# One change to a transformer block on Trainium2: chunk 0's attention scores summed on TensorE, and weighted values added up on VectorE instead of by DMA

## The chip, the cores and the metric

The kernel runs on one core of a Trainium2 chip. The metric is the device time of one execution in microseconds (us). Before the change three runs took 797.45, 798.05 and 800.79 us, with a median of 798.05.

Five engines of a core work side by side, each through its own queue, in the order of the program: TensorE (PE in the profile; PEld are its weight loads), VectorE (DVE), ScalarE (ACT), GpSimd (POOL) and SyncE (SP). SP, POOL and ACT also start DMA transfers. Semaphores make an instruction wait for those that it depends on; whatever stands behind it on its engine waits too.

## The reference

x has 2048 rows of 1024 values. The block is attention and then a feed-forward part, each with a layer norm ahead of it and a residual sum behind it. Attention is local and dilated: each row looks at itself and at the rows 2, 4, ... 14 before it (W = 8), in 32 heads of 32 values.

```python
H = 32; Dh = D // H
W, dil = 8, 2
q, k, v = ...            # layernorm(x) @ wqkv, split into heads
idx = pos[:, None] - off[None, :]
mask = idx >= 0
logits = jnp.einsum("bhsd,bhswd->bhsw", q, kg) * scale
logits = jnp.where(mask[None, None, :, :], logits, -1e9)
attn = _softmax(logits, axis=-1)
o = jnp.einsum("bhsw,bhswd->bhsd", attn, vg)
# h  = x + o @ wo
# h2 = h + ((ln(h) @ w_gate) * (ln(h) @ w_up)) @ w_down
```

`kg` and `vg` are k and v, gathered at the eight rows of each position.

## The kernel before

The 2048 rows are cut into four chunks of 512 (TC). Matrix products run on TensorE in groups of eight matmuls of 128x512, one group per 128 output columns; a group takes 1.73 us (`GROUP_US`). Results come out in PSUM, which has eight banks of 128x512 fp32 here (the pool with tag "mm"); a bank is free for a new group when the engine that reads it is done.

**Order of the groups.** `qkv(c, blocks)` is the projection of chunk c: blocks 0 and 1 are q, 2 and 3 are k, 4 and 5 are v, four groups each. The program runs, on TensorE: chunk 0's block 0, then its blocks 1 to 3; chunk 1's blocks 0 to 3; chunk 0's v; chunk 1's v; chunks 2 and 3 (L729 to L752). Then come the output projection of chunk 0 (`wo_ln2(0)`), chunk 3's v, gate and up products of chunk 0 (`ffn1(0)`), `wo_ln2(1)`, the down products of chunk 0 in two halves (`ffn2`), `ffn1(1)`, and a long second part for the remaining rows in which attention has no share, except that chunk 3's values are wanted by `wo_adds(2)` and `wo_adds(3)`.

**Layouts.** A projection group leaves 128 channels (4 heads of 32) on the partitions and 512 rows along the free dimension. `evac_qkv` (L305) has ScalarE copy it from PSUM to a tile `sg`, and SP store it to DRAM (`qd`, `kd`, `vd`). POOL loads it again (`load_qk`, `load_v`, L411 to L421) with another layout: a partition is a quarter of the chunk and a head, and the free dimensions are the 32 channels and 128 rows. The tiles `qD`, `kD`, `vD`, `oD`, `prod`, `lg` have one buffer each (pool `att`).

**Attention** (L427) is a generator. In that layout a product with a shifted window of k is one VectorE instruction over 4096 elements (L434), and the sum over a head's 32 channels is a tree of additions (L436 to L444), for two of the eight window positions at a time. Softmax follows (L446 to L462). Then v is multiplied with the weights: per pair of positions two products (L479) and one addition of the two (L483), and a DMA on POOL's queue that writes the first pair to `od` and adds each later pair to what lies there (L484). The pair's result is in `pv` (which has the buffer of `prod`) for even pairs and in `oD` for odd ones. At the end POOL loads `od` back as `oT` for the output projection (L489) and then the next chunk's v.

**What sets the order.** The program places VectorE's background work between TensorE's groups by a scheduler, `Background` (L37). After each group of 1.73 us, `bg.step` adds that much credit (4.0 us at most) and takes pieces from the first generator that is ready until the credit is spent; a `yield 2.3` charges 2.3 us, a `yield "later", 1.0` gives the turn away for 1 us. `bg.spend` charges VectorE work that the main program places itself. `bg.rate` is 1 until `wo_ln2(0)` and 0.98 from there. All this happens when the program is written out; on the chip VectorE runs its queue in that order, at whatever speed it reaches. Instructions of the main program stand in the same queue: the additions of the output projection (L514), the products of gate and up (L597), and the four stores of each half of `ffn2` (L617), all of which free or follow PSUM banks.

At the start the generators `rows_gen` (layer norms of chunks 1 and 2) are in the list; `start_attention(0)` (L737) stands after chunk 0's k and gives the generator a start 16 us later; `stats_gen(norm1[3])`, the statistics of chunk 3, is added at L736.

Of the kernel before, what the change touches and what calls it, by code (L numbers as in the profile page):

```python
# [8 lines left out]
BF = mybir.dt.bfloat16  # L9
F32 = mybir.dt.float32  # L10
I32 = mybir.dt.int32
F16 = mybir.dt.float16
ALU = mybir.AluOpType
# [7 lines left out]
DH = 32  # L21
F = 3584
W = 8
DIL = 2
HB = 16
TC = 512
NCH = S // TC
SUB = TC // 4
KO = D // 128
NF = F // 128  # L30
NP = NF // 2
EPS = 1e-5
NEG = -1.0e9
GROUP_US = 1.73


# [42 lines left out]
def kernel(  # L79
# [11 lines left out]
    nc = tc.nc  # L91
# [11 lines left out]
    t1k = ctx.enter_context(tc.tile_pool(name="t1k", bufs=30))  # L103
    small = ctx.enter_context(tc.tile_pool(name="small", bufs=4))
    att = ctx.enter_context(tc.tile_pool(name="att", bufs=1))
    psum = ctx.enter_context(tc.tile_pool(name="psum", bufs=8, space=PSUM))
# [13 lines left out]
    od = [dram.tile([4, H, DH, SUB], BF, name=f"od{c}") for c in range(NCH)]  # L120

    bg = Background()
# [4 lines left out]
        return wt, src  # L127

    stream = []
    for b in range(6):  # L130
        stream.append((("qkv", b), wqkv_v[:, :, bass.ts(b, 512)], KO))
    def stream_wo(c):
        for hf in range(2):
# [39 lines left out]
    def retire(n=1):  # L173
        state["live"] -= n
        pump()
# [116 lines left out]
    halo = const.tile([128, 16, HB], BF)  # L292
    nc.gpsimd.memset(halo[:], 0.0)
    mask = const.tile([32, W, 16], F32)
    nc.gpsimd.memset(mask[:], 0.0)
    for w in range(1, W):
        nc.gpsimd.memset(mask[:, w, 0:DIL * w], NEG)

    wps = psum.tile([128, 512], F32, tag="mm", name="warm_ps")
    for i in range(13):  # L300
# [2 lines left out]
    qkv_in = {}  # L303

    def evac_qkv(c, m, ps):  # L305
        sg = t1k.tile([128, HB + TC], BF, tag="t1k", name=f"sg{c}_{m}")
        nc.scalar.copy(sg[:, HB:HB + TC], ps[:])  # L307
        hg = m % 8
        if m >= 8:
            nc.scalar.copy(sg[:, 0:HB], halo[:, m - 8, :])  # L310
            if c + 1 < NCH:
                nc.scalar.copy(halo[:, m - 8, :], ps[:, TC - HB:TC])
        if m < 8:
            nc.sync.dma_start(qd[c][:, 4 * hg:4 * hg + 4, :, :].rearrange("c g d s -> (g d) c s"),
                              sg[:, HB:HB + TC].rearrange("p (c s) -> p c s", c=4))
            return
        dst = (kd, vd)[m // 8 - 1][c]
        base = sg[:, 0:1]
        win = bass.AP(base.tensor, base.offset, [list(base.ap[0]), [SUB, 4], [1, SUB + HB]])
        nc.sync.dma_start(dst[:, 4 * hg:4 * hg + 4, :, :].rearrange("c g d s -> (g d) c s"), win)  # L320
# [76 lines left out]
    def qkv(c, blocks, last=False):  # L397
        for b in blocks:
            for j in range(4):
                ps = psum.tile([128, TC], F32, tag="mm", name=f"ps{c}_{b}_{j}")  # L400
                mm_group(ps, wts["qkv", b], j, lnTs[c])
                evac_qkv(c, b * 4 + j, ps)
                bg.step(GROUP_US)
            if last:
                retire()
# [5 lines left out]
    def load_qk(c):  # L411
        qD = att.tile([128, DH, SUB], BF, tag="qD", name=f"qD{c}")
        kD = att.tile([128, DH, SUB + HB], BF, tag="kD", name=f"kD{c}")
        nc.gpsimd.dma_start(qD[:], qd[c].rearrange("c g d s -> (c g) d s"))
        nc.gpsimd.dma_start(kD[:], kd[c].rearrange("c g d s -> (c g) d s"))
        qkv_in["q", c], qkv_in["k", c] = qD, kD
# [7 lines left out]
        if c in stored and ("q", c) not in qkv_in:  # L424
            load_qk(c)

    def attention(c):  # L427
        qD, kD = qkv_in["q", c], qkv_in["k", c]
        lg = att.tile([128, W, SUB], F32, tag="lg", name=f"lg{c}")
        for wp in range(W // 2):  # L430
            prod = att.tile([128, 2, DH, SUB], BF, tag="prod", name=f"prod{c}_{wp}")
            for j in range(2):
                o = HB - DIL * (2 * wp + j)
                nc.vector.tensor_tensor(prod[:, j], qD[:], kD[:, :, o:o + SUB], ALU.mult)  # L434
                yield 2.3
            nc.vector.tensor_tensor(prod[:, :, 0:16], prod[:, :, 0:16], prod[:, :, 16:32], ALU.add)  # L436
            yield 2.3
            nc.vector.tensor_tensor(prod[:, :, 0:8], prod[:, :, 0:8], prod[:, :, 8:16], ALU.add)
            yield 1.2
            t3 = att.tile([128, 2, 4, SUB], F32, tag="t3", name=f"t3{c}_{wp}")  # L440
            nc.vector.tensor_tensor(t3[:], prod[:, :, 0:4], prod[:, :, 4:8], ALU.add)
            yield 1.2
            nc.vector.tensor_tensor(t3[:, :, 0:2], t3[:, :, 0:2], t3[:, :, 2:4], ALU.add)
            nc.vector.tensor_tensor(lg[:, 2 * wp:2 * wp + 2, :], t3[:, :, 0], t3[:, :, 1], ALU.add)  # L444
            yield 1.0
        if c == 0:  # L446
            nc.vector.tensor_tensor(lg[0:32, :, 0:16], lg[0:32, :, 0:16], mask[:], ALU.add)
        tr = att.tile([128, 4, SUB], F32, tag="t3", name=f"tr{c}")
        nc.vector.tensor_tensor(tr[:], lg[:, 0:4], lg[:, 4:8], ALU.max)
        nc.vector.tensor_tensor(tr[:, 0:2], tr[:, 0:2], tr[:, 2:4], ALU.max)  # L450
        mx = att.tile([128, SUB], F32, tag="mx", name=f"mx{c}")
        nc.vector.tensor_tensor(mx[:], tr[:, 0], tr[:, 1], ALU.max)
        nc.vector.tensor_tensor(lg[:], lg[:], mx[:, None, :].to_broadcast((128, W, SUB)), ALU.subtract)
        nc.scalar.activation(lg[:], lg[:], ACTF.Exp, scale=float(DH) ** -0.5)
        yield 3.5
        tr2 = att.tile([128, 4, SUB], F32, tag="t3", name=f"trs{c}")
        nc.vector.tensor_tensor(tr2[:], lg[:, 0:4], lg[:, 4:8], ALU.add)
        nc.vector.tensor_tensor(tr2[:, 0:2], tr2[:, 0:2], tr2[:, 2:4], ALU.add)
        sm = att.tile([128, SUB], F32, tag="mx", name=f"sm{c}")
        nc.vector.tensor_tensor(sm[:], tr2[:, 0], tr2[:, 1], ALU.add)  # L460
        rs = att.tile([128, SUB], F32, tag="rs", name=f"rs{c}")
        nc.vector.reciprocal(rs[:], sm[:])  # L462
        yield 2.5
        prefetch_qk(c + 1)
        while ("v", c) not in qkv_in:
            yield "later", 1.0
        vD = qkv_in["v", c]
        at = att.tile([128, W, SUB], BF, tag="at", name=f"at{c}")
        nc.vector.tensor_tensor(at[:], lg[:], rs[:, None, :].to_broadcast((128, W, SUB)), ALU.mult)
        yield 1.2  # L470
        pv = att.tile([128, 2, DH, SUB], BF, tag="prod", name=f"pv{c}")
        oD = att.tile([128, DH, SUB], BF, tag="oD", name=f"oD{c}")
        odv = od[c].rearrange("c g d s -> (c g) d s")
        for wp in range(W // 2):
            a, b = (oD[:] if wp % 2 else pv[:, 0]), pv[:, 1]
            for j, p in enumerate((a, b)):
                w = 2 * wp + j
                o = HB - DIL * w
                nc.vector.tensor_tensor(p, vD[:, :, o:o + SUB],  # L479
                                        at[:, w, None, :].to_broadcast((128, DH, SUB)), ALU.mult)  # L480
                yield 2.3
            prefetch_qk(c + 1)
            nc.vector.tensor_tensor(a, a, b, ALU.add)  # L483
            nc.gpsimd.dma_start(odv, a, max_dma_last_dim=4096,  # L484
                                accum_op=ALU.bypass if wp == 0 else ALU.add)
            yield 2.3
        oT = att.tile([128, KO, 4, SUB], BF, tag="oT", name=f"oT{c}")
        for cp in range(4):
            nc.gpsimd.dma_start(oT[:, :, cp, :], od[c][cp].rearrange("(hg hl) d s -> (hl d) hg s", hl=4))  # L489
        oTs[c] = oT  # L490
        while c + 1 < NCH and ("q", c + 1) not in qkv_in:
            yield "later", 1.0
            prefetch_qk(c + 1)
        if c + 1 < NCH:
            load_v(c + 1)
# [3 lines left out]
    def wo_ln2(c):  # L499
# [8 lines left out]
        for t in range(4):  # L508
            for hf in range(2):
# [12 lines left out]
                bg.spend(0.7)  # L522
                bg.step(GROUP_US)
        norm(3)
# [57 lines left out]
    def ffn1(c, lnT, at={}):  # L582
        hT = []
        for b in range(7):
            if b == 5 and c + 1 < NCH:
                hss[c + 1] = load_x(c + 1, "h", nc.sync)
            for j in range(4):
# [3 lines left out]
                nc.scalar.copy(gs[:], pg[:])  # L591
                bg.step(GROUP_US)
                pu = psum.tile([128, TC], F32, tag="mm", name=f"pu{c}_{b}_{j}")
# [5 lines left out]
                bg.spend(0.45)  # L599
                bg.step(GROUP_US)  # L600
                hT.append(gs)
# [120 lines left out]
    atts = {}  # L722

    def start_attention(c):
        stored.add(c)
        atts[c] = attention(c)
        bg.add(atts[c], bg.now + (16.0 if c == 0 else 0.0))

    qkv(0, range(1, 4))  # L729
    load_qk(0)  # L730
    bg.finish(rows2)
    for t in range(4):
        norm1[2].transpose(t)
    xtiles[3] = load_x(3, "x", nc.sync)
    pump(6)
    bg.add(stats_gen(norm1[3]), bg.now + 6.0)  # L736
    start_attention(0)  # L737
    qkv(1, range(4))
    qkv(0, range(4, 6))
    load_v(0)  # L740
# [85 lines left out]
    def wo_adds(c, at):  # L826
        hs = hss[c]
        for t in range(4):
            for hf in range(2):
# [5 lines left out]
                bg.spend(0.7)  # L835
                bg.step(GROUP_US)
                if 2 * t + hf in at:
# [237 lines left out]
    for q in range(4):  # L1075
        dprod(ps_x[q], q, S1, fcells(t1h), True)
        p = lnp.tile([128, TC], F32, tag="ln", name=f"dp5_{q}")
# [60 lines left out]
```

## Time and profile before

| | |
|---|---|
| median of three runs | 798.05 us |
| the profiled execution | 798.05 us |
| its span, first to last instruction | 796.2 us |
| TensorE's granted clock, mean | 0.989 of full |
| DMA moved | 146.96 MB, 185 GB/s |

Each engine's busy time over 40 slices of 19.9 us shows where it is full; a digit is tenths. A row of VectorE, for comparison with TensorE's:

```profile
DVE  5629998899988989779978429996544444478953
```

The costs of the operations that the change touches are rows of the list of groups: line, engine, operation, output and inputs, count, then busy us in total and mean ns of one, and the idle time ahead of them:

```profile
L434 DVE TENSOR_TENSOR prod<-qD,kD 128x4096 bf16<-128x4096 bf16 x32 | 72.4, 2284 | 11.5 <-DMA od<-pv 8.5
...
L479 DVE TENSOR_TENSOR pv<-vD,at 128x4096 bf16<-128x4096 bf16 x24 | 54.5, 2286 | 1.8 <-DMA od<-pv 1.7
...
L436 DVE TENSOR_TENSOR prod<-prod 128x4096 bf16<-128x4096 bf16 x16 | 36.6, 2290 | 0.4
```

A wait is read as "engine, line of the waiting instruction, what it waited for". In the order of time of one engine each row is start, duration, engine, line, operation; what stands in brackets is the idle time just before it and what ended that.

### The profile page before, as it was taken

To read this page: it belongs to the slowest core of one execution; us is meant where nothing else is said; L and a number is where in the kernel's file an instruction comes from. 1 tells how busy PE (TensorE), PEld (TensorE's weight loads), DVE (VectorE), ACT (ScalarE), POOL (GpSimd) and SP (SyncE) were. 2 spreads that over 40 slices of the span, in tenths; PEclk is the share of its full clock that TensorE was granted. 3 is DMA by queue.
4 is the path that set the end of the run, shared out by engine and by line. 5 is a ranking of instruction groups with operands and counts; after the bars stand their busy time and mean duration, and the time that the engine had idled before them with its cause. 6 is when DMAs were issued, how large, how long until landed. Compare 5 with 4: busy or idle time off the path is not lost.

```text
span 796.2 us, 10374 instructions
## 1 busy us (share of the span) xinstructions
PE 771.4 (97%) x3632; PEld 354.6 (45%) x3691; DVE 586.0 (74%) x770; ACT 471.0 (59%) x1021; POOL 157.5 (20%) x164
## 2 busy tenths in 40 slices
PE   9999999997999999994999999999999999999998
PEld 6444444443444444441444444444444444444444
DVE  5629998899988989779978429996544444478953
ACT  5626444312666642972787789855777777779140
POOL 0000001200012000002001001005877776800000
PEclk9999999999999999997999999999999999999999
DMA  8998799998999965999467976274233233550001
GB/s 284 261 246 197 173 270 193 279 293 222 304 257 255 307 245 152 266 226 321 137 186 232 259 260 187 58 167 133 74 86 105 63 98 106 190 181 28 0 27 54
DMA packets 187492, 146.96 MB, mean 185 GB/s; under 512 B 81456, under 2 KB 176688, under 8 KB 185904
## 3 DMA queue, kind: packets, MB, share of 16 engines
q1 hardware_dynamic: 176912, 110.12, 49.3%
q0 software_dynamic: 7360, 34.61, 16.6%
q10 hardware_dynamic: 3168, 1.57, 0.8%
q8 instruction: 29, 0.48, 0.3%
q14 instruction: 23, 0.19, 0.1%
HBM read 104.86 MB, written 34.60 MB: 175 GB/s over the span
## 4 chain that ended last, share of the span: by engine, by line
PE 41%; DVE 11%; DMA 3%; ACT 1%; issue 1%; SPq 0%; DVEq 0%; ACTq 0%
PE dx L787 6%; PE pz L680 6%; PE py L680 6%; PE pg L394 6%; PE px L680 6%; PE pu L394 6%; PE pv L680 3%; PE dy L787 3%; DMA lx<-in_B_w_down_dram 2%; DMA od<-pv 1%; DVE prod L434 1%; DVE h L834 1%; DVE prodx L780 1%; DVE w_dn L780 1%; DVE st L181 1%
## 5 line engine op out<-in xcount | busy, mean ns | idle before, releaser
L394 PE MATMUL ps<-lnT,w_qkv 128*128 128x512 bf16 x720 | 159.0, 379 | 3.6 <-DVE h L514 2.0
L394 PE MATMUL pg<-lnT,w_wg 128*128 128x512 bf16 x439 | 108.3, 388 | 13.9 <-DVE h L617 10.6
L394 PEld LDWEIGHTS <-w_qkv 128*128 128x128 bf16 x736 | 71.9, 98 | 89.4 <-issue 3.7
L394 PE MATMUL pu<-lnT,w_wu 128*128 128x512 bf16 x439 | 106.3, 382 | 0.5
L307 ACT CAST sg<-ps 128x512 bf16<-128x512 f32 x96 | 54.7, 589 | 50.5 <-PE ps L394 47.2
L434 DVE TENSOR_TENSOR prod<-qD,kD 128x4096 bf16<-128x4096 bf16 x32 | 72.4, 2284 | 11.5 <-DMA od<-pv 8.5
L394 PEld LDWEIGHTS <-w_wg 128*128 128x128 bf16 x448 | 44.3, 99 | 68.5 <-issue 17.5
L394 PEld LDWEIGHTS <-w_wu 128*128 128x128 bf16 x448 | 44.3, 99 | 54.2 <-issue 2.4
L680 PEld LDWEIGHTS <-sw 128*128 128x128 f16 x448 | 43.8, 98 | 53.5 <-issue 0.9
L596 ACT CAST us<-pu 128x512 bf16<-128x512 f32 x56 | 33.1, 591 | 42.6 <-PE pu L394 41.5
L479 DVE TENSOR_TENSOR pv<-vD,at 128x4096 bf16<-128x4096 bf16 x24 | 54.5, 2286 | 1.8 <-DMA od<-pv 1.7
L680 PE MATMUL px<-lnT,ws 128*128 128x512 bf16 x212 | 53.1, 379 | 0.6
L680 PEld LDWEIGHTS <-ws 128*128 128x128 f16 x336 | 32.9, 98 | 39.6
L626 PE MATMUL acc<-w_wd,gs 128*128 128x512 bf16 x220 | 48.5, 379 | 0.4 <-DVE h L514 0.2
L661 POOL TENSOR_TENSOR sw<-ws 128x512 f16<-128x512 f16 x26 | 30.0, 1153 | 84.8 <-PE py L680 77.5
L591 ACT CAST gs<-pg 128x512 bf16<-128x512 f32 x56 | 32.7, 584 | 21.5 <-PE pg L394 19.6
L185 ACT ACTIVATE rs<-mv,eps 128x1 f32<-128x1 f32 (+1 forms) x25 | 7.4, 297 | 60.3 <-DVE mv L182 55.3
L597 DVE TENSOR_TENSOR gs<-gs,us 128x512 bf16<-128x512 bf16 x56 | 23.4, 419 | 26.1 <-ACT us L596 26.0
L484 POOL DMA_DIRECT2D od<-pv x8 | 7.7, 958 | 164.6 <-DVE pv L483 128.6
L436 DVE TENSOR_TENSOR prod<-prod 128x4096 bf16<-128x4096 bf16 x16 | 36.6, 2290 | 0.4
L540 ACT ACTIVATE junkd<-w_wd 128x512 bf16<-128x512 bf16 x56 | 34.3, 613 | 0.0
L626 PEld LDWEIGHTS <-gs 128*128 128x128 bf16 x224 | 21.9, 98 | 26.8 <-issue 0.5
(313 smaller groups left out, 1383.9 us busy)
## 6 DMA issues: line engine op xcount, KB each, us to landing
w_wg<-in_B_w_gate_dram SPq DMA_DIRECT2D x14, 1024.0 KB, 9.1
w_wu<-in_B_w_up_dram SPq DMA_DIRECT2D x14, 1024.0 KB, 6.0
od<-pv POOLq DMA_DIRECT2D x8, 1024.0 KB, 8.8
od<-oD POOLq DMA_DIRECT2D x8, 1024.0 KB, 10.1
w_wd<-in_B_w_down_dram SPq DMA_DIRECT2D x8, 896.0 KB, 6.5
w_pair<-in_B_w_gate_dram SPq DMA_DIRECT2D x14, 512.0 KB, 4.0
w_pair<-in_B_w_up_dram SPq DMA_DIRECT2D x14, 512.0 KB, 5.3
w_wo<-in_A_wo_dram SPq DMA_DIRECT2D x6, 1024.0 KB, 10.2
```

Of the source, the lines that this page charges most:

```text
L307: nc.scalar.copy(sg[:, HB:HB + TC], ps[:])
L394: nc.tensor.matmul(ps[:], lhsT=wt[:, ko, bass.ts(j, 128)], rhs=rhs[:, ko, :], start=(ko == 0), stop=(ko == KO - 1))
L434: nc.vector.tensor_tensor(prod[:, j], qD[:], kD[:, :, o:o + SUB], ALU.mult)
L436: nc.vector.tensor_tensor(prod[:, :, 0:16], prod[:, :, 0:16], prod[:, :, 16:32], ALU.add)
L479: nc.vector.tensor_tensor(p, vD[:, :, o:o + SUB], at[:, w, None, :].to_broadcast((128, DH, SUB)), ALU.mult)
L540: nc.scalar.activation(junk, src, ACTF.Abs, accum_out=self.l1[:, k:k + 1])
L591: nc.scalar.copy(gs[:], pg[:])
L596: nc.scalar.copy(us[:], pu[:])
L626: nc.tensor.matmul(acc[t][:], lhsT=hT[f][:, bass.ts(t, 128)], rhs=wts["wd", c, hf, b][:, j, :], start=(f == 0), stop=(f == NF - 1))
L661: eng.tensor_tensor(sw[:, i, 0], a21, a22, ALU.add)
L680: nc.tensor.matmul(ps[:], lhsT=lhs[:, ko, :], rhs=rhs[:, ko, :], start=(fresh and ko == 0), stop=(ko == 3), skip_group_check=not fresh)
L787: nc.tensor.matmul(ps[:, bass.ds(lo, n)], lhsT=lhs[k][:, bass.ts(q, 128)], rhs=rhs[k][:, bass.ds(lo, n)], start=(fresh and k == 0), stop=( ...
```

## The change

Chunk 0's q and k are no longer stored and loaded again. ScalarE copies them from PSUM into `qT` and `kT` (in the buffers of `qD` and `kD`), channels on the partitions. `natural_logits` multiplies them on VectorE in this layout: two groups of 128 channels and four window positions in one instruction, eight instructions in all, into four buffers (two halves of `prod`, and those of `oD` and `vD`). TensorE sums over a head's channels: `heads` has a 1 where a channel belongs to a head, 32 columns wide, and each matmul (128x32 weights, 512 columns) writes 32 partitions of PSUM, one quarter of the chunk. A reduction is eight such matmuls, two channel groups by four quarters; there are eight. Reduction i is placed behind product i + 2. Two PSUM banks hold the sums until ScalarE copies them to `lg`. The window positions come in the order `NAT`, which mask and weighted values follow. Chunk 0's k block 2 is projected ahead of q block 1, its weights are loaded earlier, and attention of chunk 0 starts right behind it.

In all four chunks the weighted values are no longer added up by DMA: later pairs are added to `oD` by one more VectorE instruction each, three per chunk, and `od` is written once.

```diff
-    for b in range(6):
+    for b in (0, 2, 1, 3, 4, 5):
         stream.append((("qkv", b), wqkv_v[:, :, bass.ts(b, 512)], KO))
...
+    heads = t1k.tile([128, KO, 32], BF, tag="t1k", name="heads")
+    nc.gpsimd.memset(heads[:], 0.0)
+    for i in range(4):
+        base = heads[32 * i:32 * i + 32, 0, i:i + 1]
+        nc.gpsimd.memset(bass.AP(base.tensor, base.offset, [list(base.ap[0]), [36, KO]]), 1.0)
+    qT = att.tile([128, KO, TC], BF, tag="qD", name="qT")
+    kT = att.tile([128, KO, HB + TC], BF, tag="kD", name="kT")
+    nc.gpsimd.memset(kT[:, :, 0:HB], 0.0)
+    natural = set()
...
     def evac_qkv(c, m, ps):
+        if c == 0 and m < 16:
+            natural.add(m)
+            if m < 8:
+                nc.scalar.copy(qT[:, m, :], ps[:])
+            else:
+                nc.scalar.copy(kT[:, m - 8, HB:HB + TC], ps[:])
+                nc.scalar.copy(halo[:, m - 8, :], ps[:, TC - HB:TC])
+            return
...
+    def natural_logits(lg):
+        room = att.tile([128, 2, 2, 4, TC], BF, tag="prod", name="nprod")
+        bufs = [room[:, 0], room[:, 1], att.tile([128, 2, 4, TC], BF, tag="oD", name="nprod_o")[:],
+                att.tile([128, 2, 4, TC], BF, tag="vD", name="nprod_v")[:]]
+        acc = [psum.tile([128, 4, SUB], F32, tag="mm", name=f"lgp{i}") for i in range(2)]
+
+        def reduce(i):
+            for g in range(2):
+                hg = i // 2 * 2 + g
+                for cp in range(4):
+                    rows = slice(32 * cp, 32 * cp + 32)
+                    nc.tensor.matmul(acc[i % 2][rows], lhsT=heads[:, hg, :], rhs=bufs[i % 4][:, g, :, bass.ts(cp, SUB)],
+                                     start=(hg == 0), stop=(hg == KO - 1))
+
+        for i in range(8):
+            hg = i // 2 * 2
+            while not {hg, hg + 1, hg + 8, hg + 9} <= natural:
+                yield "later", 1.0
+            base = kT[:, hg, HB - DIL * (i % 2 * 4 + 3):HB]
+            win = bass.AP(base.tensor, base.offset, [list(base.ap[0]), [HB + TC, 2], [DIL, 4], [1, TC]])
+            nc.vector.tensor_tensor(bufs[i % 4], qT[:, hg:hg + 2, None, :].to_broadcast((128, 2, 4, TC)), win, ALU.mult)
+            yield 2.3
+            if i > 1:
+                reduce(i - 2)
+        yield "later", 2.0
+        reduce(6)
+        nc.scalar.copy(lg[:, 0:4], acc[0][:])
+        yield "later", 2.0
+        reduce(7)
+        nc.scalar.copy(lg[:, 4:8], acc[1][:])
...
         for wp in range(W // 2):
-            a, b = (oD[:] if wp % 2 else pv[:, 0]), pv[:, 1]
-            for j, p in enumerate((a, b)):
+            pv = att.tile([128, 2, DH, SUB], BF, tag="prod", name=f"pv{c}_{wp}")
+            for j in range(2):
                 w = 2 * wp + j
-                o = HB - DIL * w
-                nc.vector.tensor_tensor(p, vD[:, :, o:o + SUB],
+                o = HB - DIL * order[w]
+                nc.vector.tensor_tensor(pv[:, j], vD[:, :, o:o + SUB],
                                         at[:, w, None, :].to_broadcast((128, DH, SUB)), ALU.mult)
                 yield 2.3
             prefetch_qk(c + 1)
-            nc.vector.tensor_tensor(a, a, b, ALU.add)
-            nc.gpsimd.dma_start(odv, a, max_dma_last_dim=4096,
-                                accum_op=ALU.bypass if wp == 0 else ALU.add)
-            yield 2.3
+            if wp == 0:
+                nc.vector.tensor_tensor(oD[:], pv[:, 0], pv[:, 1], ALU.add)
+                yield 2.3
+            else:
+                nc.vector.tensor_tensor(pv[:, 0], pv[:, 0], pv[:, 1], ALU.add)
+                yield 2.3
+                nc.vector.tensor_tensor(oD[:], oD[:], pv[:, 0], ALU.add)
+                yield 2.3
+        nc.gpsimd.dma_start(od[c].rearrange("c g d s -> (c g) d s"), oD[:])
...
-        bg.add(atts[c], bg.now + (16.0 if c == 0 else 0.0))
-
-    qkv(0, range(1, 4))
-    load_qk(0)
+        bg.add(atts[c], bg.now)
+
+    qkv(0, (2,))
+    start_attention(0)
+    qkv(0, (1, 3))
...
-    start_attention(0)
```

More of the change, by code (lines that the diff above doesn't have):

```diff
@@ L33 @@
 NEG = -1.0e9
+NAT = (3, 2, 1, 0, 7, 6, 5, 4)
 GROUP_US = 1.73
@@ L295 @@
     nc.gpsimd.memset(mask[:], 0.0)
-    for w in range(1, W):
-        nc.gpsimd.memset(mask[:, w, 0:DIL * w], NEG)
+    for i, w in enumerate(NAT):
+        if w:
+            nc.gpsimd.memset(mask[:, i, 0:DIL * w], NEG)
+    heads = t1k.tile([128, KO, 32], BF, tag="t1k", name="heads")
[7 more added lines that the diff above has]
+    natural = set()
     wps = psum.tile([128, 512], F32, tag="mm", name="warm_ps")
@@ L425, in prefetch_qk, with logits @@
             load_qk(c)
-    def attention(c):
+    def natural_logits(lg):
[26 more added lines that the diff above has]
+        nc.scalar.copy(lg[:, 4:8], acc[1][:])
+    def logits(c, lg):
         qD, kD = qkv_in["q", c], qkv_in["k", c]
-        lg = att.tile([128, W, SUB], F32, tag="lg", name=f"lg{c}")
         for wp in range(W // 2):
@@ L445, in attention @@
             yield 1.0
+    def attention(c):
+        lg = att.tile([128, W, SUB], F32, tag="lg", name=f"lg{c}")
+        order = range(W) if c else NAT
+        yield from logits(c, lg) if c else natural_logits(lg)
         if c == 0:
@@ L470, in attention @@
         yield 1.2
-        pv = att.tile([128, 2, DH, SUB], BF, tag="prod", name=f"pv{c}")
         oD = att.tile([128, DH, SUB], BF, tag="oD", name=f"oD{c}")
-        odv = od[c].rearrange("c g d s -> (c g) d s")
         for wp in range(W // 2):
-            a, b = (oD[:] if wp % 2 else pv[:, 0]), pv[:, 1]
-            for j, p in enumerate((a, b)):
+            pv = att.tile([128, 2, DH, SUB], BF, tag="prod", name=f"pv{c}_{wp}")
+            for j in range(2):
                 w = 2 * wp + j
-                o = HB - DIL * w
-                nc.vector.tensor_tensor(p, vD[:, :, o:o + SUB],
+                o = HB - DIL * order[w]
+                nc.vector.tensor_tensor(pv[:, j], vD[:, :, o:o + SUB],
                                         at[:, w, None, :].to_broadcast((128, DH, SUB)), ALU.mult)
```

## The prediction

> **What bounds the kernel now.** I read the page's span and slices first, then who TensorE waited for, then the stretches around its gaps, then VectorE in order of time through the largest gap.
>
> ```profile
> span 796.2 us, 10374 instructions
> ...
> PE 771.4 (97%) x3632; PEld 354.6 (45%) x3691; DVE 586.0 (74%) x770; ACT 471.0 (59%) x1021; POOL 157.5 (20%) x164
> ...
> PE   9999999997999999994999999999999999999998
> ```
>
> TensorE is the bound: busy in every slice but two, the tenth and the nineteenth. Time can only come out of those two holes, and whatever TensorE gets in addition is paid in full. Who it waits for (engine, line, waited-for: us, times, longest):
>
> ```profile
> PE pg L394 <- DVE h L617: 10.6, 1, 10.6
> PE pg L394 <- DMA lnT<-ln: 2.9, 1, 2.9
> PE ps L394 <- DVE h L514: 2.0, 2, 1.1
> ...
> PE ps L394 <- ACT sg L307: 0.7, 1, 0.7
> ```
>
> The stretches (busy us and count of PE, PEld, DVE, ACT, POOL; then the granted clock and DMA):
>
> ```profile
> 178.80:196.90 18.10, 14.14 (x62) 6.11 (x64) 17.25 (x26) 4.93 (x18) 1.07 (x2) 0.99 0.86 212
> 196.90:200.20 3.30, 3.27 (x9) 1.19 (x10) 3.16 (x5) 0.00 (x0) 0.00 (x0) 0.52 1.02 344
> 364.80:375.40 10.60, 0.03 (x1) 0.03 (x1) 10.43 (x9) 1.62 (x3) 0.00 (x0) 0.62 1.06 314
> 375.40:381.60 6.20, 6.20 (x17) 2.20 (x17) 6.20 (x7) 0.58 (x1) 0.00 (x0) 0.55 0.80 261
> ```
>
> After each hole TensorE runs at about half clock: the next groups of eight matmuls take 3.4 us instead of 1.73. VectorE meanwhile is full. Its order of time, and its waits:
>
> ```profile
> 337.28 2.29 DVE L479 TENSOR_TENSOR oD<-vD,at 128x4096 bf16<-128x4096 bf16 x1 [4.94 <-DMA od<-oD]
> ...
> 349.16 2.29 DVE L434 TENSOR_TENSOR prod<-qD,kD 128x4096 bf16<-128x4096 bf16 x1 [5.06 <-DMA od<-pv]
> ...
> 351.37 2.48 DVE L617 TENSOR_TENSOR h<-acc,h 128x512 bf16<-128x512 f32 x4
> ...
> 374.63 2.48 DVE L617 TENSOR_TENSOR h<-acc,h 128x512 bf16<-128x512 f32 x4
> ```
>
> ```profile
> DVE oD L479 <- DMA od<-oD: 11.9, 4, 4.9
> ...
> DVE prod L434 <- DMA od<-pv: 8.5, 2, 5.1
> ...
> DVE pv L479 <- DMA od<-pv: 1.7, 1, 1.7
> ```
>
> The cause is a lag. The background scheduler places attention instructions in VectorE's queue at the pace of TensorE's groups, by nominal costs; it knows nothing of VectorE's waits for the accumulating writes to `od`. Each such wait makes VectorE later than its place in the program, and the lag stays. The second half's stores (L617) belong at TensorE's 357.7 us and run at 374.6: 17 us late. They free the PSUM banks of `acc`, so TensorE stands from 364.8.
>
> **What is there to win.** (a) Chunk 0's output projection: 16 groups of 1.73 us from 163.8 would end at 191.5; the first `pg` starts at 196.93, 5.4 late, and its eight matmuls lose 3.43 - 1.73 = 1.7 to the clock: 7.1. (b) The hole at 364.8: 10.6, then two groups in 3.37 and 2.84 instead of 1.73 each, 2.75: 13.4. (c) 0.7 at 60.1 us, where ScalarE's PSUM copies stood behind statistics of chunk 3 that waited for x. Together 21.2 us.
>
> **What the Trainium skill says.** "TensorE: Matmul & The Clock Gate", Part 1, has the half clock after an idle window of about 3.4 us; the trace agrees (0.55 after 10.6 us). Part 3 of that page says that matmuls with outputs in different 32-column groups run concurrently, 2.38 times as fast for three tiles of N=512; no instruction of this trace shows it. "TensorEngine Tiling (Array Packing)", Key Properties, says that a change of tiling mode drains the engine; also unseen here. "VectorE: DVE Perf Modes", the tier table, has bf16 `tensor_tensor` at twice the fp32 rate for step-1 operands; the trace agrees (2048 bf16 1.23 us, 1024 with an fp32 output also 1.23).
>
> **The change, part by part.**
>
> *Chunk 0's scores on VectorE.* Before: 8 products of 2.28 us, 4 adds of 2.29, and per pair 1.23 + 1.23 + 0.69 + 0.43; in the trace 10.43 us a pair, 41.7 in all. After: 8 products over 4096 bf16 elements with step 1 inside, which is L434's shape, so 8 x 2.25 = 18. VectorE loses 23.7 us of work.
>
> *The same on TensorE.* 8 reductions of 8 matmuls, 64 of N=512. Nothing hides them. Lower bound: four truly together, 64 x 0.216 / 4 = 3.5 us. Upper bound: each alone for its whole duration (379 ns, the mean of the rows), 24.3; in between, one after another but pipelined, 13.8. I take Part 3: eight matmuls on four column groups are 0.379 + 0.216 = 0.6 us, and I estimate the drain ahead of each at 379 - 216 = 0.16, so about 0.8 a reduction: 6.4 us. Do they wait for VectorE? Counting the scheduler's yields, product 0 is placed after the 11th projection group following the first block and runs as soon as VectorE is through with chunk 2's norms (38.9 us); products then end at 41.2, 43.4, 45.7, ... Reduction i is placed behind product i+2, where TensorE comes at about 42, 46 and 49. Margin 1 to 3 us, so no wait. Behind a late one would stand every projection group.
>
> *ScalarE, POOL, SP.* Eight k copies lose a halo copy; two copies of 128x512 fp32 (0.6 us each) come in; six small memsets stand on POOL's queue ahead of its 8.5 us copy, where POOL is idle from 2 us on. SP loses 16 stores of q and k, POOL the loads of `qD` and `kD`: 4.4 MB less before 60 us, so x of chunk 3 (awaited until 54.7) comes earlier. Its statistics are now placed behind the products, so (c) goes: 0.7. Two of eight PSUM banks are held by the sums for some 14 groups; the other six are 10.4 us of groups against a copy of 0.6. The new weight order costs nothing: same sizes, same queue.
>
> *Chunk 0's weighted values.* They cannot begin before V is there. Counting groups, TensorE was through with V at 81.0 and POOL issued the load at 84.6. Now this is 0.7 earlier for (c) and R later, R being the reductions' cost: 83.9 + R. The shortest landing is 6.1, and DMA is half idle at that time: V is there at 90 + R. VectorE idles from about 67 + R until then: this is where most of the 23.7 us goes. From there 15 operations of 2.245 (12 as before plus 3 adds) are 33.7; then chunk 1's scores 41.7, softmax 6.4, `at` 1.25: the first add of the output projection (L514) starts at 173 + R. TensorE asks for its bank at 177.2 + R: no wait. From that add to the first `pg` the trace shows 196.93 - 178.01 = 18.9: ready at 192 + R, where TensorE is at 190.8 + R. That is 1 us late; a landing 1 us longer than the shortest makes it 2, and I let 2 of (a)'s 7.1 stay. Bounds: 0 with V 1 us earlier; 9 with a landing of 12.6 us, the longest seen (7.6 late and the clock).
>
> *The three adds a chunk, for accumulation by DMA.* 12 adds of 2.25 = 27 us on VectorE, against 22.1 us of waits above and one of 2.9 put to issue: on VectorE's sum this is a wash. But the adds have yields, so they are charged and push later attention work back instead of making it late. POOL loses 12 of 16 writes of 1 MB, and the score products no longer wait for an accumulating write out of their own buffer. Lag in chunk 1: about 6 after the output projection as before; then no waits, 28 gate products charged 0.45 and taking 0.34, rate 0.98, so 2 to 4 at 300 us instead of 8.8. In the next 57 us before adds 10 of waits; after adds none. The second L617 runs 2 to 4 us after TensorE is there; it may be 6.9 late before a group stands. So (b), 13.4, goes. What is late next: nothing on VectorE; chunk 3's values end some 10 us later by count, at about 440, and VectorE has 2.4 us of work from 444 to 462, with the consumer at 474.
>
> **Sum.** 21.2 won, less 6.4 for reductions, less 2 left in (a): 12.8. The profiled execution is 798.05 (span 796.2 and 1.85 around it) and is itself the median of the three: 785.2; I say 785.
>
> **Rivals.** (1) Column groups run one after another, pipelined: 13.8 + 1.3 of drains: 21.2 - 15.1 - 2 = 4.1, 794. For it: nothing here shows concurrency; against: the page's 2.38. (2) VectorE stays late in chunk 0, because V lands at its longest or the reductions hold it: all of (a) stays and 2 more: 21.2 - 6.4 - 9 = 5.8, 792. For it: the wash in VectorE's sum; against: DMA is at half load at 85 us. (3) The slower side: each of the 64 matmuls is alone in the array, because weights for a column group are not loaded while another runs. At 379 ns that is 24.3 + 1.3 + 2 against 21.2: 6.4 slower, 804. It decides from (21.2 + 4 - 3.3) / 64 = 0.34 us a matmul. For it: 64 weight loads of 32 columns, one per matmul; against: 128-column loads of 98 ns are hidden in every row.
>
> **How the numbers follow.** Forecast 0.66, rival 1 0.12, rival 2 0.10, rival 3 0.12. What a measurement of this kernel can tell from no change is 0.5%, 4 us: below 794.0 is faster, above 802.0 slower. Faster: 0.66 and half of the rivals 1 and 2, some of it from the forecast's spread: 0.74. Same: 0.12. Slower 0.14: rival 3 and unseen stalls. Range: lower end 3.5 for the reductions, nothing left in (a): 780.4. Upper end takes in rivals 1 and 2: 795.
>
> **What would show it.** Right: no wait for L617; no half clock near 370; 64 matmuls of 128x32 in 8 bursts of about 0.6 us; no VectorE wait for `od`; VectorE idle between about 74 and 96. Wrong: bursts of 1.7 us or more; projection groups waiting for products between 40 and 65; a `pg` wait for `lnT` over 3 us; L617 still late.

## The result, and the profile after

Four runs took 787.24 to 790.25 us, with a median of 788.76; the kernel before, beside them, 797.75 (797.23 to 800.79). The ratio is 0.988, 95% interval 0.985 to 0.991: 9 us less, where 13 were forecast, and inside the forecast's range of 780 to 795. The profiled execution took 787.24, its span is 785.5, 10.7 us shorter than that of before.

The page of the changed kernel: the span, the busy time of each engine, and the slices of TensorE and VectorE.

```profile
span 785.5 us, 10418 instructions
...
PE 772.2 (98%) x3695; PEld 354.0 (45%) x3755; DVE 590.1 (75%) x762; ACT 472.8 (60%) x1015; POOL 142.0 (18%) x156
...
PE   9999999999899999999999999989999999999998
...
DVE  5794099999999999998899349985544534478853
```

The two holes of TensorE, a 7 and a 4 before, are gone; an 8 and another 8 are left (the last 8 was there before). VectorE's 0 in the fifth slice is its wait for V. Who TensorE waits for, in the same columns as before:

```profile
PE pg L413 <- DMA lnT<-ln: 2.9, 1, 2.9
PE pv L737 <- DVE h L849: 2.3, 2, 2.1
```

The wait for the second half's stores (10.6 us) is no longer listed, that for `lnT` is as long as it was, and one behind VectorE's `h` has grown from 0.2 to 2.3. TensorE in the stretch in which it stood before, and VectorE in order of time, at V's landing and at the stores of the second half (L674 is what L617 was):

```profile
358.00:375.40 17.40, 17.29 (x80) 7.94 (x81) 15.05 (x16) 10.46 (x21) 0.00 (x0) 1.00 0.59 189
```

```profile
96.88 4.50 DVE L531 TENSOR_TENSOR pv<-vD,at 128x4096 bf16<-128x4096 bf16 x2 [19.52 <-DMA vD<-vd]
...
359.66 2.48 DVE L674 TENSOR_TENSOR h<-acc,h 128x512 bf16<-128x512 f32 x4
```

TensorE begins the group behind `acc` at 358.46; the stores follow 1.2 us later, where they were 17 us late. The granted clock of this stretch is 1.00, where 0.62 and 0.55 stood. So hole (b) and its half clock, 13.4 us, are gone. The end of hole (a), the first `pg`, is still late, but at full clock:

```profile
199.61 1.89 PE L413 MATMUL pg<-lnT,w_wg 128*128 128x512 bf16 x8 [2.85 <-DMA lnT<-ln]
```

The reductions, in TensorE's order of time (a row of `lgp` is one reduction, `ps` are projection groups of eight):

```profile
42.71 0.61 PE L457 MATMUL lgp<-nprod,heads 128*32 128x512 bf16 x8
43.26 3.63 PE L413 MATMUL ps<-lnT,w_qkv 128*128 128x512 bf16 x16
46.81 0.61 PE L457 MATMUL lgp<-nprod,heads 128*32 128x512 bf16 x8
```

From the first burst's start to the next group 0.55 us pass, and the two groups in between take 3.55 from start to start, where 16 matmuls at 0.216 are 3.46. A reduction thus costs 0.64, eight of them 5.1. The start of chunk 0's output projection fits: 168.70 against 163.69 before is 5.0, and with the 0.7 of (c), which was gained ahead of it, 5.7. Of these, 0.5 was there before the first reduction: TensorE's first full projection group starts at 17.55 instead of 17.08, behind a longer warm-up (5.72 us instead of 5.10). That leaves 5.2.

| where the 10.7 us of span come from | us |
|---|---|
| (b), the hole behind the second half's stores, and its half clock | +13.4 |
| (c), ScalarE's copies at 60 us | +0.7 |
| (a), chunk 0's output projection: `pg` 3.2 late instead of 7.1 with the clock | +3.9 |
| reductions on TensorE | -5.2 |
| the later start of the first full group | -0.5 |
| the new wait near 529 us (2.3 in place of 0.2) | -2.1 |
| sum | 10.2 |

Half a microsecond is left over. The 3.2 is 199.61, where `pg` starts, less 196.4, where the 16 groups of 1.73 from 168.70 on would end.

### The profile page after: what moved, and what is told of

Its sections match the earlier page's. It is cut to its first block, busy times and chain, and to the rows that moved or that the text cites. A ratio compares the mean times of both kernels' runs of the same rounds, so it can differ in the third digit from the quotient of the medians.

```text
span 785.5 us, 10418 instructions
## 1 busy us (share of the span) xinstructions
PE 772.2 (98%) x3695; PEld 354.0 (45%) x3755; DVE 590.1 (75%) x762; ACT 472.8 (60%) x1015; POOL 142.0 (18%) x156
## 4 chain that ended last, share of the span: by engine, by line
PE 79%; DVE 15%; DMA 3%; ACT 1%; issue 1%; ACTq 0%; DVEq 0%
PE pg L413 12%; PE pu L413 12%; PE ps L413 8%; PE dx L844 6%; PE pz L737 6%; PE acc L683 6%; PE py L737 6%; PE px L737 6%; PE wo L889 3%; PE pv L737 3%; PE dy L844 3%; DVE pv L531 3%; DVE prod L483 2%; PE wo L569 2%; PE ex L844 2%; DVE prod L485 1%
## 5 line engine op out<-in xcount | busy, mean ns | idle before, releaser
L413 PE MATMUL pg<-lnT,w_wg 128*128 128x512 bf16 x438 | 105.0, 379 | 3.4 <-DMA lnT<-ln 2.9
L531 DVE TENSOR_TENSOR pv<-vD,at 128x4096 bf16<-128x4096 bf16 x32 | 72.5, 2286 | 19.7 <-DMA vD<-vd 19.5
L326 ACT CAST sg<-ps 128x512 bf16<-128x512 f32 x80 | 46.9, 588 | 64.6 <-PE ps L413 62.9
L483 DVE TENSOR_TENSOR prod<-qD,kD 128x4096 bf16<-128x4096 bf16 x24 | 54.4, 2285 | 0.1
L543 POOL DMA_DIRECT2D od<-oD x4 | 2.2, 542 | 254.7 <-DVE oD L541 254.7
L648 ACT CAST gs<-pg 128x512 bf16<-128x512 f32 x56 | 32.6, 582 | 16.6 <-PE pg L413 14.2
L737 PE MATMUL pv<-prodx,sw 128*128 128x512 f16 x112 | 28.7, 379 | 2.3 <-DVE h L849 2.3
L754 ACT COPY py<-px 128x512 f32<-128x512 f32 x28 | 16.0, 570 | 24.3 <-PE px L737 24.3
```

The lines of the kernel that those rows point to most:

```text
L413: nc.tensor.matmul(ps[:], lhsT=wt[:, ko, bass.ts(j, 128)], rhs=rhs[:, ko, :], start=(ko == 0), stop=(ko == KO - 1))
L531: nc.vector.tensor_tensor(pv[:, j], vD[:, :, o:o + SUB], at[:, w, None, :].to_broadcast((128, DH, SUB)), ALU.mult)
L737: nc.tensor.matmul(ps[:], lhsT=lhs[:, ko, :], rhs=rhs[:, ko, :], start=(fresh and ko == 0), stop=(ko == 3), skip_group_check=not fresh)
```

## The experiments

Two theories were to be told apart. The *charge theory*: the holes are a lag of VectorE's queue, made by waits for accumulating writes that the scheduler doesn't know of; the additions help because they put known, charged time in the place of unknown waits, and the new scores do little. The *work theory*: what helps is that the scores take some 24 us of work from VectorE.

**Each part alone.** First the new scores with the accumulation by DMA put back:

```diff
-                nc.vector.tensor_tensor(oD[:], oD[:], pv[:, 0], ALU.add)
-                yield 2.3
-        nc.gpsimd.dma_start(od[c].rearrange("c g d s -> (c g) d s"), oD[:])
+            nc.vector.tensor_tensor(a, a, b, ALU.add)
+            nc.gpsimd.dma_start(odv, a, max_dma_last_dim=4096,
+                                accum_op=ALU.bypass if wp == 0 else ALU.add)
+            yield 2.3
```

> The change with its second part undone: chunk 0's scores stay summed on TensorE, the weighted values go back to accumulation by DMA in all chunks. Charge theory (the holes come from VectorE's waits for the accumulating writes, which the scheduler does not charge): the hole behind the second half's stores comes back, 10 us or more of waiting for L-of-the-stores, and the wait for lnT ahead of the first gate product grows from 2.9 to about 8, because chunk 0 begins its values only at 97 us and then waits for DMA again: 804 to 810, slower than the kernel before. Work theory (the holes went because the scores take 24 us of work off VectorE): no hole, 786 to 792.

804.46 us (803.61 to 804.68) against 797.59: ratio 1.008, interval 1.006 to 1.011. The new scores alone make the kernel slower, so the work theory falls. The hole was not where it had been expected, though: not behind the second half's stores, but at chunk 0's output projection. TensorE's longest wait, and ScalarE in order of time at that place:

```profile
PE wo L566 <- ACT sg L326: 11.4, 1, 11.4
```

```profile
180.53 1.06 ACT L508 ACTIVATE lg<-lg 128x1024 f32<-128x1024 f32 x1 [22.89 <-DVE lg L507]
```

VectorE lags already in chunk 1, and that meets ScalarE first: an exponential of chunk 1's softmax waits 22.9 us for VectorE, the copies of chunk 3's projection stand behind it in ScalarE's queue, no PSUM bank comes free, and the output projection stops from 170.7 to 182.1. A lag is paid where the first bank hangs on it; this need not be VectorE's own consumer.

Then the additions alone, with the scores as they were before:

> The change with its first part undone: chunk 0's scores as before, on VectorE and with q and k stored and loaded; the weighted values are added on VectorE, charged to the scheduler. Charge theory: no hole behind the second half's stores (13.4 us), the lag at chunk 0's output projection is less by the 5.5 us of DMA waits that chunk 0 had, so the wait for lnT all but goes (7.1 us), and TensorE is spared the 5.6 us of reductions: 776 to 781, faster than both. Work theory: VectorE has 27 us more work than before and nothing taken off, so holes stay: 796 or more.

777.47 us (777.15 to 777.79), ratio 0.974 (0.971 to 0.978), clock 1.0. It is faster than the kernel before and the changed one. Of the 21.2 us that the prediction hoped to win, 20.3 are in the span. TensorE's longest waits, and VectorE's stores of the second half:

```profile
PE warm_ps L301 <- DVE warm L287: 1.2, 1, 1.2
PE ps L394 <- ACT sg L307: 1.1, 1, 1.1
```

```profile
354.69 2.48 DVE L620 TENSOR_TENSOR h<-acc,h 128x512 bf16<-128x512 f32 x4
```

No wait above 1.2 us is left. The additions are the whole gain, and on top of them the new scores cost 11.3 us (788.76 less 777.47). In the spans of the profiled executions it is 9.6: the reductions, the later start, the rest of (a) and the wait near 529 us, less these 1.1 us behind ScalarE's copies, which the new scores take away.

**Is it the work of the additions or their charge?** The kernel before, with accumulation by DMA and no addition, is given only the charge, one line:

```diff
                                 accum_op=ALU.bypass if wp == 0 else ALU.add)
             yield 2.3
+            if wp:
+                yield 2.3
```

> The kernel before with nothing but one more charge of 2.3 us in the scheduler for each of the second to fourth pairs of a chunk; the instructions are the same, the accumulation stays with the DMA. Charge theory: attention work is placed later by what VectorE waits, so the stores are not behind it any more: no hole at 365 us, lnT in time, 776 to 782. Rival (the waits for DMA themselves cost time, whatever the order): 795 to 800, hole still there.

784.07 us (782.39 to 784.94), ratio 0.982 (0.978 to 0.986). Both holes are gone with no instruction of VectorE or DMA added or removed, only with another order. It comes out 2 us above what was expected. These waits are left, of TensorE and then of VectorE:

```profile
PE ev L789 <- DVE es L911: 2.3, 1, 2.3
PE wo L834 <- ACT ep L932: 1.9, 1, 1.9
PE pv L682 <- DVE h L794: 1.6, 2, 1.4
```

```profile
DVE prod L434 <- DMA od<-pv: 11.6, 3, 4.8
DVE oD L479 <- DMA od<-oD: 11.0, 4, 5.1
DVE prodx L770 <- DMA prodx<-in_B_w_down_dram: 3.9, 1, 3.9
```

VectorE still waits 24 us for accumulating writes (with one more wait, of 1.7), where it was 22 before. These waits are now allowed for. But chunk 3's last write takes 12.5 us to land and holds the buffer of `oD` until 466.4, where the last write of the additions alone takes 8.8; and the load of `prodx`, into the buffer of `prod`, lands 16.6 us after its issue instead of 8.6. That these two make up what is missing is argued here; for the buffer of `oD` it is tried further down.

The opposite test: the additions stay and their charge goes, in the version with the additions alone and in the changed kernel:

```diff
                 nc.vector.tensor_tensor(oD[:], oD[:], pv[:, 0], ALU.add)
-                yield 2.3
```

> The faster variant with the scores of before and the weighted values added on VectorE, without the charge (yield 2.3) for each chunk's three new additions; the instructions are the same. Charge theory: each chunk makes VectorE 6.75 us later than its places in the program, so lnT is late again by about 6 us plus 1.7 of clock, and at the second half's stores the lag is some 16 us, a hole of 9 to 10 plus 2.8 of clock: 793 to 800, all of the gain lost. Rival (what helped is that the accumulating writes are gone): 777 to 779.

> The changed kernel without the charge (yield 2.3) for each chunk's three new additions; the instructions are the same. Charge theory: lnT is late by 10 us instead of 3, or ScalarE's copies stand that long behind chunk 1's exponential, and a hole of up to 9 us comes back behind the second half's stores: 800 to 810. Rivals (the work off VectorE, or the writes that are gone, made the gain): 788 to 790.

793.1 us (792.4 to 794.21) with the additions alone, ratio 0.993 (0.991 to 0.996): 15.6 slower than with the charge. And 802.47 (802.33 to 802.87) for the changed kernel, 1.005 (1.003 to 1.007): this line of Python decides whether it is faster or slower than before. The waits of the two, in that order:

```profile
PE pg L394 <- DVE h L619: 4.3, 1, 4.3
PE pg L394 <- DMA lnT<-ln: 2.8, 1, 2.8
PE ps L394 <- DVE h L516: 2.8, 1, 2.8
```

```profile
PE wo L568 <- ACT sg L326: 7.3, 1, 7.3
PE acc L682 <- DVE h L570: 4.0, 4, 2.0
```

The first list has the two waits of the kernel before again (`pg` for `h`, `pg` for `lnT`), without a single accumulating write; the second has the wait behind ScalarE's copies that the scores alone showed. VectorE time that the scheduler doesn't count makes the holes, whether it is waiting or work.

The charge is not all of the gain, though. Against the kernel before, measured beside each, the bare charge brings 13.5 us, the additions without their charge 6.2, and both together 20.1. So about two thirds come from the charge and a third from having additions in the place of accumulating writes; what makes up that third was not taken apart.

**Are the column groups concurrent because of their order?** In the changed kernel the two loops of a reduction are exchanged: for each channel group all four column groups before, for each column group its two channel groups now.

```diff
-            for g in range(2):
-                hg = i // 2 * 2 + g
-                for cp in range(4):
+            for cp in range(4):
+                for g in range(2):
+                    hg = i // 2 * 2 + g
```

> The changed kernel with the two loops of a reduction exchanged, so that two matmuls on the same 32 columns follow each other. If column groups do run side by side only because neighbours in the queue are on different columns: a burst grows from 0.61 to about 1.1 to 1.3 us, eight of them add 4 to 5 us, less what the wait for lnT gives back (VectorE's lag does not change, so up to 0): 791 to 794. If order in the queue does not matter: 0.61 and 788.8.

788.63 us (787.99 to 789.19), no different from the changed kernel. The bursts take the same time:

```profile
46.50 0.62 PE L457 MATMUL lgp<-nprod,heads 128*32 128x512 bf16 x8
```

Two matmuls on the same columns, one right behind the other in the program, do not serialize a burst. In both orders the trace has four of the eight matmuls start within 0.03 us and the other four 0.23 us after them.

**What is left of (a).** In the changed kernel chunk 0's values are placed at the time at which V is asked for, and VectorE then waits 19.5 us for V. One wait in the schedule is added to the generator, behind its test that V has been projected:

```diff
         while ("v", c) not in qkv_in:
             yield "later", 1.0
+        if c == 0:
+            yield "later", 8.0
```

> The changed kernel, with chunk 0's weighted values placed 8 us later in the program, about when V has landed, not when its load is issued. If the wait for lnT (2.9 us in the profile, with a dip of the clock in some runs) is VectorE's lag from V's landing: the wait goes, the runs come closer together, 784.5 to 786.5. If it is something else (the transposes, ScalarE): 788 to 789.

783.38 us (783.3 to 783.89), ratio 0.981 (0.979 to 0.983): 5.4 better than the changed kernel (3.8 between the spans of the profiled executions) and 1.1 better than expected. TensorE no longer waits for `lnT`, and its first `pg` is at 196.21. The last of the layer norm's instructions of chunk 0, in the changed kernel and then here:

```profile
195.76 0.55 DVE L191 TENSOR_SCALAR ln<-h,mv,rs 128x1024 bf16<-128x1024 bf16 x1 [0.60 <-ACT rs L187]
```

```profile
188.91 0.55 DVE L191 TENSOR_SCALAR ln<-h,mv,rs 128x1024 bf16<-128x1024 bf16 x1 [0.60 <-ACT rs L187]
```

They run 6.9 us earlier although V lands at the same time (VectorE takes it up at 97.20 against 96.88). The wait for V is the same; what differs is that the order of VectorE's queue allows for it: the first addition of the output projection runs at 173.41, ahead of most of chunk 1's softmax, and not at 180.71 behind all of it. These runs also lie closer together, at mean clocks of 0.999 to 1.0; those of the changed kernel have 0.995 to 1.0. The profiled execution of the exchanged loops, at 0.998, shows what can happen after the wait for `lnT`:

```profile
199.80 3.35 PE L413 MATMUL pg<-lnT,w_wg 128*128 128x512 bf16 x8 [2.88 <-DMA lnT<-ln]
```

After the same wait as in the changed kernel (2.88 against 2.85 us) the clock is 0.57 here, the eight matmuls take 3.35 us instead of 1.89, and the span is 1.7 us longer. With the later values the wait is gone.

**A last microsecond, and a deadline.** In the version with the additions alone TensorE still waits 1.1 us for ScalarE's copies, which stand behind statistics of chunk 3. These were placed 8 us later:

```diff
-    bg.add(stats_gen(norm1[3]), bg.now + 6.0)
+    bg.add(stats_gen(norm1[3]), bg.now + 14.0)
```

> The scores of before and the additions on VectorE, charged, and also chunk 3's statistics placed 8 us later, behind the landing of x, so that ScalarE's copies do not stand behind them. The wait of 1.1 us at 60 us goes if that is its cause: 776 to 777. If not: 777.5.

785.41 us (784.5 to 786.08): 8 slower, where up to 1 faster was expected. The microsecond is there (the first `pg` starts at 190.9 instead of 192.0), but TensorE stands later, behind ScalarE:

```profile
PE wo L835 <- ACT ep L933: 5.8, 1, 5.8
```

```profile
471.23 3.28 ACT L769 ACTIVATE ox<-ox,sbd 128x3584 f16<-128x3584 bf16 x1 [2.01 <-DMA ox<-in_B_w_down_dram]
478.66 3.28 ACT L769 ACTIVATE lx<-lx,sbd 128x3584 f16<-128x3584 bf16 x1 [4.14 <-DMA lx<-in_B_w_down_dram]
```

In the new order the last addition of chunk 3 ends at 456.8 instead of 453.7. It frees `oD` for the store to `od`, and only behind that store can down weights for the second part, `ox`, be loaded into the same buffer. The load is issued at 466.4 instead of 462.9, that of `lx` behind it in SP's queue at 466.8 instead of 463.3, and this one lands after 11.9 us instead of 6.8. ScalarE works in order, so `ep` is 7 us late (487.42 against 480.42). In the run with the bare charge `ox` was issued at 466.6 and `lx` landed after 12.2: its 1.9 us of waiting for `ep` are the same wait.

To test that, the third addition is left uncharged in chunk 3 alone, so that its last products and additions come earlier:

```diff
                 nc.vector.tensor_tensor(oD[:], oD[:], pv[:, 0], ALU.add)
-                yield 2.3
+                if c < 3:
+                    yield 2.3
```

> Before's scores, adds on VectorE, statistics of chunk 3 placed 8 us later (the version that came out at 785.4), and the third addition of each pair is not charged in chunk 3 alone, so that chunk 3's last products and additions stand some 4 us earlier in VectorE's queue. Nothing is left out. Deadline theory (the 8 us that version lost are a load of down weights, ox, that cannot start until chunk 3's sum has left its buffer oD, and ScalarE and TensorE stand behind it near 485): the load of ox starts 3 to 4 us earlier against TensorE, no wait of wo for ep, 776.0 to 777.5, as fast as the version without the later statistics or up to 1 us faster. Rival (the later statistics cost the time elsewhere, as by an unlucky place of the clock or the other transfers): it stays at 784 to 786. Second rival (two additions uncharged make VectorE late for the gate products before 450 us): 778 to 784, with TensorE waiting for gs or us there.

779.15 us (778.94 to 779.25), ratio 0.976 (0.974 to 0.978): 6.3 of the 8 us are back. `ox` is issued at 464.7, `lx` lands after 7.0, and the wait for `ep` is gone:

```profile
PE ex L791 <- DVE w_dn L772: 1.1, 1, 1.1
PE ex L791 <- DVE gs L601: 0.6, 1, 0.6
```

So there is a deadline: when the last addition of chunk 3 comes earlier, the wait goes. Why `lx` lands so much later is not shown, since in this version the loads of `oT`, which POOL issues behind it, also come 2.0 us later (469.1 instead of 467.1). What is missing to the expected 776.0 to 777.5 is the second rival: two uncharged additions make VectorE late for TensorE by 1.7 us near 450. None of the later versions beats the additions alone, at 777.5.

## Why the prediction was right, and where it was off

**(b), the hole of 13.4 us: right in size and cause.** Stores 2 to 4 us behind TensorE were forecast, 1.2 was measured. That it was the charge, and not the shorter scores, is shown from both sides: the bare charge closes the hole without any other change, and without the charge waiting for these stores returns, 4.3 us with the additions alone and 1.6 in the changed kernel, which then pays 7.3 earlier, at chunk 0's output projection.

**(c), 0.7: right.** No copy of ScalarE holds TensorE at 60 us.

**The reductions, 6.4: 5.2 measured.** The burst of 0.6 us was right to a hundredth (0.61). The Trainium skill, "TensorE: Matmul & The Clock Gate", Part 3, gives 2.38 for three column tiles; here eight matmuls on four column groups take 0.61 where eight full ones take 1.73 to the next group, 2.8 times as fast at least, so the trace agrees. The drain was too dear: 0.16 us for each was estimated from a pipelined matmul's tail, the groups in between show 0.09; and 0.76 a reduction was rounded up to 0.8. "TensorEngine Tiling (Array Packing)", Key Properties, says that a change of the mode drains the engine; these 0.09 us are what is left for it here. Rivals 1 and 3, serial column groups and matmuls alone, needed bursts of 1.7 and 3 us and fall. No reduction waited for its product, as forecast.

**What stays of (a), 2: 3.2 measured.** The chain of steps was right; one term of it was too small. The forecast had `lnT` ready at 192 + R and TensorE there at 190.8 + R. With the measured 5.7 for R (the later start included) that is 197.7 and 196.5. TensorE would have been there at 196.4, but `pg` could start only at 199.6, 1.9 later than 197.7. Of this, 1.0 is V's landing (7.1 us, not the shortest 6.1), which the forecast had allowed for. The term that was mis-sized is that of the fifteen value operations: 34.5 us from the first of them to the next score product, 2.30 each with the step from one to the next, where 2.245 and 33.7 were counted. That is 0.8. From there on everything agrees, to the 18.9 us between the first addition and `pg`. That VectorE returned from V at 96.88, where 96.4 was forecast, is in part luck: the load was issued 0.6 sooner and took 1.0 longer. Rival 2 stood for this at its worst (all of (a) stays, 792); in the profiled execution about half stays.

**Not foreseen: 2.1 us near 529 us.** TensorE waits there for `h`. Ahead of it, from 510 on, ScalarE's `lnr` rows wait 2.6 us in two waits for transposes of earlier rows, which the kernel before doesn't show. The changed kernel, the exchanged loops and the later values all have both waits (2.2 to 2.6), and the scores alone and the changed kernel without its charge have 1.9 and 1.3; the additions alone have none. In the changed kernel the third to fifth of the eight transposes land after 4.0 to 4.9 us, with the additions alone after 3.2 to 3.3. But the bare charge shows 1.6 us of the same wait of TensorE without ScalarE's. What makes the transposes slow was not tried and stays open.

**The sum, 12.8: 10.7 in the span, 9 between the medians.** Against the forecast the span is 1.2 better in the reductions, 0.5 worse by the later start, 1.2 worse in (a) and 2.1 worse in the new wait, which makes 10.2. The terms missed in both directions, and part of what they missed cancels. The other runs of the changed kernel are up to 3 us longer than the profiled one. Two of them have the mean clock of the traced execution of the exchanged loops, 0.998, so half clock behind the wait for `lnT`, 1.7 us there, is the likely reason; the slowest, at 0.995, has no trace to compare. The prediction held the idle window of the half clock against the gap of 10.6 us alone. Gaps shorter than that window were enough here, but not always: half clock followed gaps of 2.86 us (before) and 2.88 (exchanged loops), and did not follow 2.85 (changed kernel) and 2.81 (additions uncharged).

**What the prediction left unsaid** is that its own terms priced the two parts with opposite signs. All but the 0.7 of (c) of the 21.2 us came with the additions; the scores brought 6.4 of cost on the engine that sets the time, and a relief of VectorE that, as it also said, would mostly be spent waiting for V. With the rows side by side its own numbers give about 777.5 for the additions alone (798.05 less 20.5, an estimate in hindsight); 777.47 was measured.

## What to carry to other kernels

Where a program's order is written out ahead by nominal costs, look for time that the costs don't hold, and charge it, before removing any work: here one line closed holes that 24 us less of vector work left open, and one line less brought them back. Price each part of a change apart, on the engine that sets the end: work taken from an engine with a wait ahead is turned into waiting, while the work put on the bound is paid in full. When a schedule moves by 2 or 3 us, look for the next buffer that must be free in time, since a load that was issued 1.7 us later there landed 6.6 us later.

## What the runs showed of the hardware that was not expected

- Order doesn't matter in a burst of column-tiled matmuls: 0.61 us for eight over four column groups, 0.62 with the two of one column group side by side. The Trainium skill, "TensorE: Matmul & The Clock Gate", Part 3, says that matmuls start and end in the order of the program. With the loops exchanged this doesn't fit the trace, if the same columns take one matmul at a time: starting in order, at 0.216 us from one to the next on the same columns, a burst's last matmul could start only after 4 x 0.216 = 0.86 us, and 0.55 us after the burst's start the next group has begun. The records don't say which columns a matmul is on, so which of the two gives is open.
- In the kernel before an accumulating DMA write of 1 MB took about twice as long as a plain one of the same size: the twelve accumulating writes landed 8.4 to 11.7 us after their issue (median 9.9), the four plain ones after 4.4 to 9.1 (median 4.8). Plain writes took 5.5 in the median in the changed kernel, but 8.4 with the additions alone, so accumulation isn't all that counts.
- The load of `lx` landed after 6.8 and 7.0 us when issued at 463.3 and 465.1, and after 11.9 and 12.2 when issued at 466.8 and 467.0: 1.7 us later at the start were 6.6 at the end. In the two slow cases the four loads of `oT` (1 MB in all) begin 0.3 and 2.0 us behind it, in the two fast ones 4.9 and 4.0. That it shares the transfer with them is likely and was not tried; in the changed kernel, where it is issued within 3 us of `prodx` and `ox` and long before `oT`, it took 11.9 as well.
